# Twelve pieces of unread matrix products in a replaced order of work, in an attention and gMLP kernel on one core

## The chip, the cores and the metric

The kernel runs on one core of a Trainium2 chip. The metric is the device time of one execution in microseconds (us), as the median of several. A profile of one further execution gives the span from the first instruction to the last one and the time of every instruction on every engine.

The engines are named as in the profile: PE is TensorE (its matmuls), PEld the loading of PE's weights, DVE is VectorE, ACT is ScalarE, POOL is GpSimd and SP is SyncE, which here issues transfers only. Each engine runs its own list of instructions strictly in the order in which the program gives them, and waits on semaphores for the others.

## The reference

Inputs are q, k and v of shape 4 x 8 x 768 x 64 (batch, heads, positions, head size) and the weights of a gated MLP. For each head the 768 keys are cut into 24 chunks of 32. Of each chunk the smallest and largest value per dimension give an upper bound on the score of a query:

```python
ub = np.sum(np.maximum(q[:, :, :, None, :] * k_min[:, :, None, :, :], q[:, :, :, None, :] * k_max[:, :, None, :, :]), axis=-1)
causal = pos[:, None] // chunk >= np.arange(nc)[None, :]
ub = np.where(causal, ub, -1000000000.0)
top_chunks = np.argsort(ub, axis=-1)[..., -top_k:]
```

Each query then attends, causally, only to the keys of its six best chunks, with an ordinary softmax. The 128 queries of the first tile reach four chunks at most, so that none of theirs is ever left out. The eight heads side by side (512 numbers a position) go through the MLP: `h = max(x @ w_in, 0)`, the second half of `h` normalised per position and mixed over positions by a 768 x 768 matrix plus a bias, multiplied by the first half, and then by `w_out`. The output is 4 x 768 x 512 in float32.

## The kernel before

The work is done for 16 pairs of heads, p = 0 to 15, four for each of the four batches; the pair's two heads lie on the two halves of the 128 partitions. After the four pairs of a batch b comes the MLP of that batch. All of it is cut into some 1400 named pieces, each a few instructions on one engine. `work_list` (L251 to L461) lists each piece with its engine (or the two that may do it), a planner's cost in us, the pieces that it comes after, and the buffers that it takes new or uses. A function `k_<name>` writes each piece's instructions. The pieces that matter here, in the order of one pair:

- `load` (L626) brings k, q, v in; `cast` (L635) makes them 16 bits wide; `turn` (L648) transposes k or q on PE, six matmuls of 128 columns; `kT`, `qT` (L661, L674) copy the result out of PSUM and `qp` (L679) makes max(-q, 0). From the fifth pair on transfers on SP do the transposing.
- `ext` (L666): two DVE reductions that give each chunk's largest and smallest key values.
- `bounds` (L692): PE forms the upper bounds of all queries with all chunks, for six tiles of 128 queries and both heads, in matmuls of 24 columns. For the first six pairs (`EARLY`) a product of `big` and `far`, which marks the chunks that lie ahead, is added as one more matmul; for the others DVE adds it in `ub`.
- `ub`, `top`, `leave` (L704 to L725): the bounds are copied out, DVE finds the eight largest of each row, and marks what is left out. `top` reads the bounds of tiles 1 to 5 only. In `leave` the first tile's threshold is a constant which lies between the mark of a chunk ahead and any bound.
- `pk`, `mx` (L770, L792): scores with keys across, and their largest per chunk by DVE reductions, so that the softmax knows what to subtract. For the first three pairs part of that is folded: `kd` on POOL, `fd`, `fi`, `fb` on PE and `fr` on ACT.
- `minus`, `kept`, `shift`, `turn_bias`, `bT`: the bias of each query and chunk, transposed by PE in six matmuls that use half of the array's rows each (L826).
- `probs`, `ex` (L843, L867): scores with queries across plus the bias on PE, exponential on ACT, in six slices. `cut` (L874) on POOL clears what lies ahead in the diagonal blocks, once for each head.
- `weigh` (L880) multiplies by v on PE; `av`, `sum`, `inv`, `norm` (L888 to L916) copy out and divide; `turn_x`, `xT` transpose for the MLP.

The MLP of a batch is `hv`, `vr`, `bn`, `rstd`, `vn` (the half that is normalised), `hu`, `uT` (the other one), `mix`, `ms` or `plus`, `gT` (mixing over positions and gating), and `og`, `oe`, `od` (last product, copy out, store).

Two things set the order. **The order of the pieces** comes from `Work.order` (L114 to L215), which runs while the program is built: it plays the work through with the costs of the list, and on each engine takes of the pieces that are ready the one with the lowest number in the table `RANK`. `WHERE` gives one letter for each piece that could go to two engines. **PE's two ways of use**: pieces of the kinds in `TILED` (L100) have matmuls on 64 rows, two of which run side by side; the others use all 128 rows. The planner adds 0.095 us where PE goes from one kind to the other.

PSUM holds three double buffers of tag `two` and two single ones of tag `mg`. A piece that takes a buffer waits until the last reader of the one before is done.

At the start the first load of k goes to ACT's queue and all others to SP's. POOL makes constants (`ident`, `far`, `rows`), DVE fills others (`clear`, `zero`, `small`, `halves`), and PE has nothing to do until the first `turn`.

Of the kernel before, what the change touches and what calls it, by code (L numbers as in the profile page):

```python
# [16 lines left out]
P = 128  # L17
# [15 lines left out]
0 9 100 7 13 10 5 1 28 103 118 168 128 124 256 303 296 313 298 327 425 450 446 421 430 435 398 407 417 422 403 411 388  # L33
396 381 391 2 11 3 12 4 44 14 16 20 23 17 19 21 27 32 35 38 43 39 41 54 29 22 25 24 31 40 47 55 61 71 66 37 42 48 51
60 56 65 68 77 102 112 115 119 125 130 136 159 163 146 151 135 143 150 155 145 171 178 152 177 180 186 196 199 209 214
15 49 8 34 36 82 58 63 79 107 46 57 52 123 132 139 147 140 148 149 154 72 70 75 73 84 89 105 138 144 153 158 87 90 101
108 114 116 111 160 165 172 179 183 187 193 202 204 213 224 218 230 195 200 216 221 217 242 250 228 253 258 263 270
274 284 292 6 26 18 53 80 113 30 33 45 50 64 69 74 81 85 93 99 98 94 106 129 59 83 88 157 161 169 173 184 190 197 194
76 78 95 109 122 126 120 141 208 215 236 239 247 254 257 262 271 276 278 281 266 267 268 273 269 300 306 283 290 308
315 332 335 347 354 67 92 62 86 96 134 104 110 133 142 91 117 97 227 231 237 240 249 244 243 255 166 170 191 238 251  # L40
164 176 252 259 198 201 203 207 282 285 261 293 299 311 314 317 324 334 338 343 349 328 331 337 342 330 336 344 358
364 350 369 377 382 387 392 414 418 121 156 127 174 175 233 162 167 181 188 182 185 189 205 212 219 222 223 225 220
229 232 235 245 260 264 294 302 275 279 304 312 287 291 288 295 241 319 339 353 360 365 372 393 399 423 439 420 427
374 380 413 416 415 483 488 408 497 506 514 526 529 552 131 192 137 211 246 305 226 272 277 234 286 297 301 309 345
310 346 321 352 307 318 323 355 359 322 326 409 419 362 371 340 348 432 437 361 442 452 465 467 475 479 493 500 509
518 507 511 535 549 489 492 520 561 568 513 566 575 582 584 587 595 210 265 206 248 329 402 280 333 341 289 316 351
356 366 367 368 375 370 378 379 384 389 434 440 405 412 445 455 397 400 401 404 386 394 385 459 468 482 486 548 578
593 600 574 585 606 610 571 592 627 630 647 658 667 626 668 682 691 714 739 749 320 357 325 373 390 454 363 424 429
395 460 521 527 534 539 536 538 541 572 463 470 477 558 562 461 480 554 559 504 510 496 499 487 494 577 583 594 634
641 649 656 655 662 672 678 687 693 663 669 681 685 686 723 730 713 728 733 742 746 748 763 383 438 376 428 474 543  # L50
443 503 517 433 498 532 545 551 576 557 553 555 580 519 523 530 540 547 591 601 636 645 565 569 666 670 612 617 588
680 688 705 708 711 719 731 745 736 741 761 767 718 725 751 756 765 776 783 759 781 789 798 812 818 827 406 471 410
481 528 590 564 605 611 544 598 623 628 635 637 643 639 652 657 609 615 622 651 659 701 710 750 754 638 648 675 679
625 632 770 777 790 804 807 817 822 832 838 811 825 857 863 829 845 831 836 842 889 897 847 905 917 930 935 939 949
516 550 522 567 619 785 631 664 674 644 673 683 694 698 717 699 720 702 732 690 697 703 715 721 768 772 760 764 753
757 860 867 738 743 794 876 882 909 915 938 944 950 953 942 947 962 970 977 984 960 965 975 996 1003 1002 1013 1020
1028 1032 1066 1077 581 665 573 653 726 795 696 727 735 707 737 766 769 778 786 784 782 780 808 775 787 799 846 856
868 873 773 803 788 793 883 890 885 895 814 899 920 972 978 985 989 1004 1011 1000 1006 993 997 1019 1023 1034 1039
1038 1050 1057 1043 1055 1061 1071 1079 1084 1093 661 774 654 734 821 888 779 813 834 771 802 844 852 861 866 865 880
881 918 879 886 898 900 907 982 986 1007 1010 896 904 954 958 995 999 922 1024 1030 1049 1052 1062 1069 1067 1074 1078  # L60
1091 1083 1087 1075 1082 1094 1100 1098 1109 1113 1092 1105 1117 1122 1133 1136 1144 797 837 792 826 892 927 864 913
925 874 919 951 956 963 964 971 966 968 979 911 923 936 1045 1056 967 974 1017 1025 991 994 941 946 914 931 1080 1104
1115 1127 1131 1138 1142 1148 1153 1151 1156 1166 1175 1157 1163 1172 1179 1158 1198 1203 1165 1202 1208 1211 1213
1216 1222 810 853 816 870 926 1108 983 1005 1018 990 1014 1031 1037 1044 1047 1060 1064 1048 1072 1026 1033 1041 1170
1174 1095 1101 1042 1051 1059 1065 1159 1164 1103 1107 1076 1182 1194 1197 1201 1218 1221 1238 1245 1207 1227 1236
1240 1205 1224 1251 1254 1256 1263 1269 1250 1270 1274 1276 1279 1281 1288 908 1012 912 952 1063 1112 1040 1073 1088
1054 1081 1099 1110 1118 1160 1121 1150 1134 1168 1111 1120 1126 1185 1196 1191 1200 1181 1186 1116 1137 1183 1189
1114 1123 1177 1206 1212 1235 1237 1242 1248 1267 1272 1252 1257 1258 1264 1255 1261 1266 1271 1275 1283 1287 1280
1285 1290 1291 1293 1295 1302 1305 436 444 447 441 449 458 478 484 491 451 457 462 469 476 485 456 464 473 502 505 515
524 560 570 546 563 537 426 431 490 495 466 472 512 531 501 508 542 556 448 453 525 533 586 599 602 613 596 604 607  # L70
640 579 589 597 616 642 650 660 671 618 624 692 724 603 608 621 633 629 646 709 729 614 620 676 700 706 712 722 677
684 689 695 704 716 740 747 806 755 762 801 744 752 758 791 800 823 835 841 848 805 815 820 796 809 828 824 833 839
819 830 843 855 859 872 875 906 903 894 878 891 840 850 862 869 851 858 849 854 871 884 877 887 902 910 893 901 916
924 932 957 973 980 988 998 933 940 948 959 955 976 981 992 928 934 943 1008 945 961 1016 1053 987 1001 1027 1058 921
929 937 969 1036 1046 1068 1022 1029 1035 1009 1015 1021 1070 1086 1089 1090 1097 1106 1085 1096 1102 1119 1125 1130
1124 1129 1147 1145 1149 1155 1141 1146 1152 1128 1135 1139 1132 1140 1143 1162 1169 1178 1184 1204 1190 1209 1214
1195 1154 1167 1192 1199 1210 1217 1176 1188 1215 1219 1173 1180 1187 1193 1161 1171 1229 1232 1233 1220 1225 1234
1243 1249 1260 1223 1228 1239 1226 1230 1244 1259 1265 1268 1246 1253 1262 1231 1241 1247 1277 1284 1286 1292 1298
1299 1300 1304 1306 1273 1278 1282 1289 1294 1296 1297 1301 1303 1307 1309 1311 1310 1315 1317 1308 1312 1314 1313
1318 1320 1316 1321 1324 1319 1325 1329 1323 1326 1332 1335 1340 1336 1334 1337 1344 1346 1347 1348 1322 1328 1333  # L80
1341 1345 1351 1327 1331 1338 1343 1330 1339 1349 1353 1342 1350 1358 1361 1362 1352 1355 1365 1354 1357 1366 1356
1359 1363 1369 1375 1379 1360 1368 1371 1364 1370 1374 1367 1372 1377 1380 1385 1387 1376 1382 1384 1373 1378 1381
1389 1393 1394 1386 1391 1392 1383 1388 1390
"""
WHERE = """
AAAAGAGAGVGVGAAVAGAGAGVVAGAGAGAVVVVVAVAVAAAAAVVAVGGGGVGGAAVAAAAAAAAAAAVVAVAVVAAVAAVVGGGGGVVAAAAA
# [3 lines left out]
class Work:  # L90
# [8 lines left out]
    DELAY = {"PE": 0.25, "DVE": 0.17, "ACT": 0.18, "POOL": 0.14, "SP": 0.0}  # L99
    TILED = ("pk", "probs", "bounds", "turn_bias", "fd", "fb")  # L100
# [12 lines left out]

    def order(self):  # L114

        pieces, n = self.pieces, len(self.pieces)
        users, slot, freed_at, done_at = {}, {}, {}, {}
        slots = {tag: [None] * k for tag, k in self.bufs.items()}
        then, todo, ready_at, begun = [[] for _ in range(n)], [0] * n, [0.0] * n, [False] * n
        for i, (_, _, _, after, new, old, _) in enumerate(pieces):  # L120
            for b in new + old:
                users[b] = users.get(b, 0) + 1
            for a in after:
                then[self.index[a]].append(i)
                todo[i] += 1
        rank, where = [int(x) for x in RANK.split()], iter(WHERE.replace("\n", ""))
        engine = dict(P="PE", V="DVE", A="ACT", G="POOL", S="SP")
        assert len(rank) == n
        for i, (name, on, _, after, new, old, dma) in enumerate(pieces):
            if len(on) > 1:  # L130
                e = engine[next(where)]
                on = {e: on[e]}
# [934 lines left out]
```

## Time and profile before

| | before |
|---|---|
| median of 3 runs | 249.05 us (248.89 to 249.26) |
| the profiled execution's own time | 248.22 us |
| its span | 246.5 us |
| PE busy, matmuls | 224.9 us of it, 3780 instructions |
| DVE busy | 206.5 us, 512 instructions |
| ACT busy | 191.9 us, 298 instructions |
| POOL busy | 165.9 us, 209 instructions |
| moved by DMA | 35.51 MB |

A busy time is the sum of stretches in which the engine had an instruction under way. Matmuls overlap, so PE can be busy throughout and still have pauses between starts. In a row of the timeline or of the groups, "L807 DVE" is line 807 of the kernel before and its engine, "cmax<-two" the tile written and the one read, "x2" the count. In the chain of waits a row gives the start, the length, and what the end of the program waited for at that time.

### The profile page before, as it was taken

The page shows a single profiled execution, that of the slowest core. Times are in us where ns is not written, and L with a number is a line of the kernel's source. Part 1 is how long each engine was busy: PE and PEld are TensorE (multiplying, and loading weights), DVE is VectorE, ACT ScalarE, POOL GpSimd, SP SyncE. Part 2 cuts the span into 40 slices and gives each one's busy share as a digit, 9 for nine tenths or more (in the row PEclk, how much of TensorE's full clock was granted, in tenths as well). Part 3 has the DMA queues.
Part 4 walks back from the last instruction along what each step waited for, and adds up shares of the span by engine and source line. Part 5 has one row for each costly group of instructions (what it writes and reads, how often), then busy time and mean ns, then how long its engine had stood idle before and what let it go on. Part 6 is the DMA issues. An engine that isn't in the chain of part 4 may idle for free.

```text
span 246.5 us, 9019 instructions
## 1 busy us (share of the span) xinstructions
PE 224.9 (91%) x3780; PEld 144.6 (59%) x3780; DVE 206.5 (84%) x512; ACT 191.9 (78%) x298; POOL 165.9 (67%) x209
## 2 busy tenths in 40 slices
PE   0898778878999999999999999999999999999993
PEld 0656457666755675666665576666745566645551
DVE  4799999999999999799998997899998853349670
ACT  3598887979998999587859897897679969767312
POOL 8879749887785377999965929999926147402160
PEclk9999999999999999999999999999999999999999
DMA  7969996699999949484899997128900010350005
GB/s 189 325 186 201 257 242 127 122 164 241 168 186 235 216 82 187 89 170 112 190 161 271 175 200 125 34 75 140 268 22 19 0 36 0 105 188 0 0 28 227
DMA packets 93895, 35.51 MB, mean 144 GB/s; under 512 B 86208, under 2 KB 90144, under 8 KB 93856
## 3 DMA queue, kind: packets, MB, share of 16 engines
q1 hardware_dynamic: 91568, 31.81, 61.9%
q0 software_dynamic: 2016, 2.75, 6.5%
q8 instruction: 29, 0.48, 0.8%
q10 hardware_dynamic: 272, 0.39, 0.5%
q14 instruction: 10, 0.08, 0.1%
HBM read 24.77 MB, written 6.29 MB: 126 GB/s over the span
## 4 chain that ended last, share of the span: by engine, by line
PE 48%; DVE 28%; ACT 14%; DMA 4%; issue 3%; POOL 2%; DVEq 0%; ACTq 0%
DVE cmax L807 11%; PE mg L1001 11%; ACT pr L871 8%; PE mg L1024 6%; PE mg L885 5%; PE two L856 4%; PE mg L937 3%; PE two L863 3%; DVE stats L954 3%; DVE ext L671 3%; PE two L786 3%; DVE top L715 2%; PE mg L990 2%; DMA k<-in_k_dram 2%; DVE cmax L801 2%
## 5 line engine op out<-in xcount | busy, mean ns | idle before, releaser
L871 ACT ACTIVATE pr<-two 128x1024 f16<-128x1024 f32 (+1 forms) x96 | 85.3, 934 | 5.4 <-PE two L863 4.8
L807 DVE TENSOR_REDUCE cmax<-two 128x24 f32<-128x768 f32 (+4 forms) x104 | 85.3, 843 | 3.5 <-PE two L735 2.0
L856 PE MATMUL two<-qT,kT 64*128 64x128 f16 (+3 forms) x384 | 40.5, 258 | 5.4 <-ACT bT L835 1.9
L863 PE MATMUL two<-bT,member 64*128 64x128 f16 (+1 forms) x512 | 39.7, 233 | 0.0
L877 POOL TENSOR_SCALAR_AFFINE_SELECT pr<-pr 128x768 f16<-128x768 f16 x32 | 27.9, 886 | 9.1 <-ACT pr L871 9.0
L1019 POOL TENSOR_TENSOR vr<-tmp,uT 128x384 f16<-128x384 f32 x27 | 24.5, 922 | 11.9 <-DVE tmp L1012 11.8
L671 DVE TENSOR_REDUCE ext<-kT 128x24 f16<-128x768 f16 x32 | 29.5, 936 | 1.9 <-ACT kT L617 1.7
L1001 PE MATMUL mg<-wsT,vn 128*128 128x384 f16 x168 | 30.2, 327 | 0.0
L856 PEld LDWEIGHTS <-kT 64*128 64x128 f16 x384 | 19.9, 94 | 17.2 <-issue 15.1
L863 PEld LDWEIGHTS <-member 64*128 64x128 f16 x512 | 25.7, 94 | 5.1
L885 PE MATMUL mg<-v,pr 128*128 128x65 f16 x672 | 25.9, 194 | 0.7 <-POOL pr L877 0.5
L786 PE MATMUL two<-kT,qT 64*128 64x384 f16 (+4 forms) x182 | 24.6, 280 | 1.4 <-ACT pr L871 0.5
L885 PEld LDWEIGHTS <-pr 128*128 128x128 f16 x672 | 23.1, 98 | 3.6 <-issue 1.0
L1001 PEld LDWEIGHTS <-vn 128*128 128x128 f16 x192 | 17.7, 98 | 12.2 <-issue 0.6
L990 PE MATMUL mg<-xT,w_in_sb 128*128 128x384 f16 x112 | 22.4, 328 | 0.0
L907 POOL TENSOR_TENSOR x<-av,rc 128x768 f16<-128x768 f32 x11 | 16.2, 1469 | 8.8 <-DVE rc L900 4.9
L732 PE MATMUL two<-kT,qT 64*128 64x128 f16 x192 | 19.6, 221 | 2.3 <-ACT qT L617 1.0
L1024 PE MATMUL mg<-w_out_sb,vr 128*128 128x512 f16 x84 | 20.8, 380 | 0.0
L937 PE MATMUL mg<-w_in_sb,xT 128*128 128x512 f16 x84 | 20.3, 380 | 0.4 <-DVE o L619 0.4
L889 ACT COPY av<-mg 128x390 f32<-128x390 f32 x32 | 15.6, 500 | 6.2 <-PE mg L885 6.0
L954 DVE BATCH_NORM_STATS2 stats<-vr 128x6 f32<-128x512 f32 x24 | 16.6, 692 | 4.0 <-ACT vr L942 2.9
L735 PE MATMUL two<-half_ahead,ident 64*128 64x64 f16 x192 | 19.8, 193 | 0.0
(113 smaller groups left out, 496.8 us busy)
## 6 DMA issues: line engine op xcount, KB each, us to landing
q<-in_q_dram SPq DMA_DIRECT2D x16, 384.0 KB, 6.4
v<-in_v_dram SPq DMA_DIRECT2D x16, 384.0 KB, 5.7
out_dram<-o SPq DMA_DIRECT2D x24, 256.0 KB, 2.1
k<-in_k_dram SPq DMA_DIRECT2D x15, 384.0 KB, 5.7
vr<-in_moe_w_spatial_dram POOLq DMA_DIRECT2D x6, 192.0 KB, 5.6
w_in_sb<-in_moe_w_in_dram POOLq DMA_DIRECT2D x4, 256.0 KB, 8.8
w_out_sb<-in_moe_w_out_dram POOLq DMA_DIRECT2D x4, 128.0 KB, 4.5
k<-in_k_dram ACTq DMA_DIRECT2D x1, 384.0 KB, 4.7
```

What stands on the lines that cost most here:

```text
L671: nc.vector.tensor_reduce(held["ext", p][:, m], src, axis=AX.X, op=Alu.min if m else Alu.max, negate=(m == 1))
L786: mm(t[:, h, o:o + before], lhsT=qT[rows[h], c], rhs=kT[rows[h], a * CH:a * CH + before], start=True, stop=True)
L807: nc.vector.tensor_reduce(tops(p)[:, i // 2, :, i % 2, a:z], held["two", (p, u)][:, :, o:o + n].rearrange("p h (c e) -> p h c e", e=CH), a ...
L856: mm(t[:, h, z:z + n * P], lhsT=kT[rows[h], keys], rhs=qT[rows[h], i * P:(i + n) * P], start=True, stop=False)
L863: mm(d, lhsT=member[rows[h], r, keys], rhs=bT[rows[h], m * P:(m + w_) * P].rearrange("c (m s) -> c m s", s=P), start=False, stop=(n == 1 o ...
L871: nc.scalar.activation(out=held["pr", p][:, :, c0:c0 + n], in_=held["two", (p, "e", c0)][:, :, 0:n], func=Act.Exp, scale=scale)
L877: nc.gpsimd.affine_select(out=d, in_=d, compare_op=Alu.is_ge, fill=0.0, base=0, channel_multiplier=-1, pattern=[[0, NT], [1, P]])
L885: mm(a[:, i, :], lhsT=pr[:, at[t, i]:at[t, i] + P], rhs=vp[:, h * NT + t, :], start=(t == 0), stop=(t == i))
L937: mm(t, lhsT=held["xT", b][:, ko, i * P:(i + 1) * P], rhs=w_in_sb[:, ko, DH:2 * DH], start=(ko == 0), stop=(ko == NDO - 1))
L990: mm(t, lhsT=w_in_sb[:, ko, db * P:(db + 1) * P], rhs=held["xT", b][:, ko, s * HS:(s + 1) * HS], start=(ko == 0), stop=(ko == NDO - 1))
L1001: mm(t, lhsT=held["vn", b][:, si, db * P:(db + 1) * P], rhs=wsT[:, si, s * HS:(s + 1) * HS], start=(si == 0), stop=(si == NT - 1))
L1024: mm(t, lhsT=held["vr", ("g", b)][:, ko, i * P:(i + 1) * P], rhs=w_out_sb[:, ko, :], start=(ko == 0), stop=(ko == KO - 1))
```

## The change

- **Unread products.** A piece `spark` on DVE fills a tile of 128 x 512 with ones. Twelve pieces `warm`, each three matmuls of 128 rows by 512 columns with these ones, write PSUM buffers of tag `mg` that nobody reads.
- **The order.** `RANK` is a new table, and now holds each piece's place itself: nothing is played through any more. `WHERE` is new as well. A buffer goes to the one of its tag that has been out of use longest. A few planner costs differ (`norm`, `plus`, `gT`, `bn`, `rstd1`, `bounds`).
- **The first tile's bounds.** For tile 0 only the product of `big` and `far` is made, for all pairs; the three products with the keys are left out.
- **`turn_bias`.** Where both neighbours on PE use all rows, its matmuls take all 128 rows too (pairs 1, 4, 10 and 14).

PE's list begins so (before on the left, changed on the right):

```
turn 0 k            warm 11, 7, 2, 6
turn 0 q            turn 0 k
pk 0,0              warm 4
pk 0,1              turn 0 q
bounds 0            warm 8, 5
turn 2 k            pk 0,0
fd 0,1              bounds 0
fd 0,0              pk 0,1
turn 1 q            turn 2 k, fd 0,1, fd 0,0
fi 0,1              warm 0, 9
fb 0,1              fi 0,1
```

`warm` 3, 10 and 1 follow at places 25, 29 and 31 of PE's list (counted from 0), between pieces of pairs 1 and 2. SP's list begins with q of pair 0, then k and q of pair 2, q and k of pair 1, and only then v of pair 0, which stood second before. On DVE `ub` of pairs 0 and 1 is new, and `ub` of pairs 3 and 4 has gone to ACT. `norm` of pairs 7 and 11 goes from POOL to DVE, `norm` of 13, 14 and 15 from DVE to POOL. Some pieces of the last two MLPs change engines as well.

```diff
-    for i in range(NT):   # k_bounds
-            each = [(big, far[:, i])] * (p < EARLY) + [(qT[:, c], x[:, 0]), (qp[:, c], x[:, 0]), (qp[:, c], x[:, 1])]
+            each = [(big, far[:, i])] * (p < EARLY or i == 0) + [(qT[:, c], x[:, 0]), (qp[:, c], x[:, 0]), (qp[:, c], x[:, 1])] * (i > 0)
...
+    w.add(("spark",), {"DVE": 0.3}, -10)
+    for x in range(WARM):
+        w.add(("warm", x), {"PE": 0.64}, -9 + 0.4 * x, after=[("spark",)], new=[("mg", ("warm", x))])
...
+    def k_spark(e):
+        nc.vector.memset(spark, 1.0)
+
+    def k_warm(e, x):
+        t = new("mg", ("warm", x), [P, 512], F32)
+        for n in range(3):
+            mm(t, lhsT=spark[:, 0:P], rhs=spark, start=True, stop=True)
...
+        rank, where = [int(x) for x in RANK.split()], iter(WHERE.replace("\n", ""))
...
+        for (name, on, _, _, _, _, _), at in zip(pieces, rank):
+            result[at] = name, engine[next(where)] if len(on) > 1 else next(iter(on)), at
...
+                free = [(-1 if x is None else last[x], k) for k, x in enumerate(tenants) if x is None or users[x] == 0]
+                slot[b] = min(free)[1]
...
-                mm(t[:, g, m * D:(m + 1) * D], lhsT=bias[slot["bias", p]][r, 4 * m:4 * m + 4, :].rearrange("p g c -> p (g c)"), rhs=ident[r, r], start=True, stop=True)
+                if p in whole:
+                    r, c = c, r
+                mm(t[:, g, m * D:(m + 1) * D], lhsT=bias[slot["bias", p]][r, 4 * m:4 * m + 4, :].rearrange("p g c -> p (g c)"),
+                   rhs=ident[r, c] if p in whole else ident[r, r], start=True, stop=True)
```

## The prediction

> **What bounds the kernel now.** I read the page first, then the busy time by stretches, then the chain of waits in order of time, and last the timeline of the first 16 us.
>
> ```profile
> span 246.5 us, 9019 instructions
> PE 224.9 (91%) x3780; PEld 144.6 (59%) x3780; DVE 206.5 (84%) x512; ACT 191.9 (78%) x298; POOL 165.9 (67%) x209
> PEclk9999999999999999999999999999999999999999
> ```
>
> The profiled execution took 248.22 us, 1.7 more than its span. The median of the runs is 249.05, 0.83 above it. I make the sum against 248.22 and add 0.83 at the end. PE is the busiest, but over the whole span this says little, since stages differ. Columns: us of the stretch, then busy time of PE, PEld, DVE, ACT, POOL.
>
> ```profile
> 0.00:7.80 7.80, 1.46 (x12) 1.20 (x12) 3.02 (x20) 2.92 (x4) 6.29 (x19) 1.00 0.79 217
> 7.80:20.00 12.20, 10.68 (x249) 7.62 (x250) 11.79 (x26) 9.43 (x14) 9.97 (x13) 1.00 0.84 231
> 20.00:40.00 20.00, 16.13 (x378) 11.58 (x375) 19.23 (x57) 18.02 (x25) 14.75 (x23) 1.00 1.09 232
> 40.00:60.00 20.00, 16.64 (x454) 12.84 (x450) 19.96 (x54) 17.33 (x26) 16.54 (x23) 1.00 0.87 155
> 60.00:80.00 20.00, 19.78 (x310) 12.65 (x308) 19.18 (x42) 18.18 (x29) 14.32 (x19) 1.00 1.20 201
> 80.00:100.00 20.00, 19.72 (x381) 13.20 (x378) 19.40 (x53) 19.09 (x32) 12.84 (x14) 1.00 0.92 164
> 180.00:200.00 20.00, 19.92 (x234) 10.99 (x233) 15.86 (x38) 18.99 (x33) 7.22 (x8) 1.00 0.11 22
> ```
>
> There are three stages. Until 7.8 us all wait for the first k. From 7.8 to 60 DVE is the bound: of 52.2 us it is idle for 0.41 + 0.77 + 0.04 = 1.2, while PE is idle for 8.8. From 60 on PE is busy almost throughout, in the first 40 us of it together with DVE and ACT. Whatever shortens PE's work before 60 us is worth nothing there, unless it brings work to DVE earlier.
>
> **The clock of PE.** The page's clock row and the clock column of the stretches (the 1.00) show full speed throughout. The timeline contradicts them at the start:
>
> ```profile
> 1.02 0.70 DVE L576 MEMSET member<- 128x768 uint32 x1 [1.02 <-PEq L1051]
> 6.14 0.82 PE L652 MATMUL mg<-ident,k 128*128 128x128 f16 x6 [6.14 <-DVE k L619]
> 7.00 0.80 ACT L617 COPY kT<-mg 128x768 f16<-128x768 f16 x1 [1.06 <-PE mg L652]
> 7.69 0.81 ACT L617 COPY qT<-mg 128x768 f16<-128x768 f16 x1
> 7.83 1.81 DVE L671 TENSOR_REDUCE ext<-kT 128x24 f16<-128x768 f16 x2 [1.75 <-ACT kT L617]
> 8.55 0.29 PE L732 MATMUL two<-kT,qT 64*128 64x128 f16 x2 [0.95 <-ACT qT L617]
> 9.55 1.81 DVE L795 TENSOR_REDUCE cmax<-two 128x24 f32<-128x768 f32 x2
> 12.29 0.80 PE L652 MATMUL mg<-ident,q 128*128 128x128 f16 x6
> 15.05 0.50 PE L652 MATMUL mg<-ident,k 128*128 128x128 f16 x6
> ```
>
> The same six transposes take 0.82 at 6.14, 0.80 at 12.29 and 0.50 at 15.05. So PE is slow until some time between 13.1 and 15.05; it needed at most 15.05 - 8.55 = 6.5 us of nearly unbroken work, counted from its last long pause. The difference of 0.32 is 0.053 for 128 columns, so 0.21 for 512. A 512-column matmul at full speed takes a quarter of the 0.86 below, 0.215; slow, I estimate 0.43.
>
> ```profile
> 10.01 0.64 PE two L702 x48
> 112.59 0.97 PE mg L1024 x4
> 151.79 1.08 PE mg L1001 x6
> 153.43 0.44 PE two L702 x36
> 160.54 0.77 PE mg L885 x21
> 163.40 0.66 PE mg L885 x21
> 229.76 0.97 PE two L1001 x6
> 239.29 0.86 PE mg L1024 x4
> ```
>
> **Unread products and the first stage.** Each piece is 3 x 0.215 = 0.65 us at full speed, 1.28 slow (estimates). `spark` fills 512 halves; `clear` fills 1536 in 0.70, so about 0.3. It ends at 1.3, and DVE's fills, late by as much, end long before DVE's cast of k at 5.5. PE can start at 1.5. Four pieces stand before the first transposes, one between k's and q's, two before `pk` 0,0.
>
> Say the clock rises after 6.3 us of work, the upper end from the rows: at 7.8. Then the four pieces end at 1.5 + 5.1 = 6.6, the k transposes at 7.25 (before 6.96 with their tail), and kT is copied from 7.4 instead of 7.00: +0.4 for `ext`. `warm` 4 and q's transposes follow until 8.5, qT is copied from 8.7 to 9.5, `warm` 8 and 5 end at 9.8, and `pk` 0,0 gives DVE its first `mx` at 10.35 instead of 9.55: **+0.8**. If the clock rises by 5.7, the four pieces end before 6.14; k's transposes take 0.5, kT comes 0.3 earlier, and `warm` 8 and 5 then hold `pk` until 8.8, which at full speed still delivers by 9.35: **-0.2**. So ahead of DVE the pieces gain 0.2 or lose 0.8. What they give later is that PE, fast from then on, feeds DVE without pauses. DVE's idle time from 7.8 to 60 is 1.2 us, and no more than that can go. The five later pieces, 3.2 us of PE, lie where PE waits for `fr` or for DVE, with 8.8 us idle to hide them; without that cover they would cost their 3.2. `bounds` 0 now precedes `pk` 0,1 and waits for the second `ext`; behind it on PE stands only `pk` 0,1, for which DVE's `mx` comes after `ub`.
>
> ```profile
> L619 DVE COPY ub<-two 128x288 f32<-128x288 f32 x2 | 0.9, 446 | 0.0
> L907 POOL TENSOR_TENSOR x<-av,rc 128x768 f16<-128x768 f32 x11 | 16.2, 1469 | 8.8 <-DVE rc L900 4.9 <-ACT bT L835 3.3 <-ACT pr L871 0.3
> L907 DVE TENSOR_TENSOR x<-av,rc 128x768 f16<-128x768 f32 x5 | 5.0, 996 | 0.1
> ```
>
> Two `ub` of 0.45 come to DVE and two leave it within the stage: nothing. I take +0.8 for the start and -0.8 of the 1.2 idle: **0**, with ends of -1.4 and +0.8. v of pair 0 is now behind four more loads on SP's queue, but POOL's cast of it stands later as well, and its first reader is `weigh` 0 after 30 us.
>
> Here a page of the Trainium skill can be weighed. "TensorE: Matmul & The Clock Gate", section "Part 1: The HAM clock gate", says that the array runs at half speed until a free-running window of about 3.4 us has been busy. By that rule the pieces from 1.5 us on would open the gate between 4.9 and 8.3, and the start would be worth -0.2 to about +1.1 in place of +0.8. The rows agree on the halving (0.82 against 0.50); that 8.55 to 13.1 did not suffice here is slower than the section's typical 4 us.
>
> **First tile's bounds.** For pairs 0 to 5, 6 of 48 matmuls go: 6/48 x 0.64 = 0.08 each, all in the stage where PE has time: 0. For the other ten, 4 of 36: 4/36 x 0.44 = 0.05 each, **-0.5** in the stage where PE is full.
>
> **Fewer changes of PE's use.** A group followed by the other kind lasts longer: `og` 0.97 against 0.86, `mix` 1.08 against 0.97, `weigh` 0.77 against 0.66, so 0.11 for a change. Counting the two orders, PE changes 172 times before and 168 times after; from `turn_x` of pair 2 on (58.7 us) 140 times and 128. The 12 that go, 1.3 us, lie almost all between 59 and 127 us, and in 60 to 100 DVE and ACT are as full as PE. I count half: **-0.65** (0 to -1.3). `turn_bias` on all rows is in the count: six matmuls of 64 columns one after another, where two and two ran side by side: by 64/128 of the 0.056 of a fast transpose (0.50 for six, with their tail) a loss below 0.1 each.
>
> **The end of pair 15.** PE waits there twice:
>
> ```profile
> 211.52 2.50 POOL pr L877 x2
> 214.06 0.84 PE mg L885 x21
> 214.90 3.48 PE mg L1024 x16
> 218.41 0.70 DVE o L619
> 219.15 1.89 PE mg L937 x8
> ```
>
> `weigh` 15,1 waits for the two `cut`, because slice 512 of `probs` 15 came last; 1.33 us lie between the starts of 15,0 (212.73) and 15,1 (214.06) where 0.66 would do. The new order puts that slice before both `weigh` of pair 14, but then slice 1024 comes late, and ACT's exponential of it ends about 0.4 too late by the same counting: -0.3. Then `norm` 15 goes to POOL, 1.47 for 1.00, and only three `og` (2.6 us) instead of four cover it. From `weigh` 15,1 on: copy, sum and reciprocal end after 1.85 as before, `norm` after 3.4, the transposes start after 3.5 and the copy of xT ends after 4.9; the fourth `og` runs beside that copy. `hv` 3 starts after 4.95 instead of 219.15 - 214.06 = 5.09: -0.15. Together **-0.5** (+0.2 to -0.8). From `hv` 3 on both orders run PE without a pause, and the last store follows a copy on ACT in both.
>
> **Other waits.**
>
> ```profile
> PE two L856 <- DVE cmax L807: 0.9, 2, 0.5
> PE two L786 <- DVE cmax L807: 0.2, 1, 0.2
> ```
>
> These are the first and the last of six rows on which PE waits after 55 us, 3.0 us in all. A new order of every engine may have none of them or as many again: 0, ends -3 and +3.
>
> **Sum.** 0 - 0.5 - 0.65 - 0.5 = -1.65. The profiled execution would come to 248.22 - 1.65 = 246.6, the median to **247.4**. Its own range, by half of the ends: 246.1 to 248.5.
>
> **Rivals.**
> 1. *The products stand in the way* (slower). If the clock rises late, all seven early pieces run slow: four end at 6.6, k's transposes at 7.25, `warm` 4 and q's at 9.2, `warm` 8 and 5 at 11.7, `pk` 0,0 delivers at 12.5 instead of 9.55: DVE is 3.0 us late, in a stage in which it is the bound. That gives 247.4 + 3.0 = 250.4, about 249.9 with some idle time regained. It outweighs the gains from a rise after some 9.5 us on. For it: counted from the first matmul (6.14) the rise took up to 8.9 us, which from 1.5 would be 10.4. Against: PE paused for 0.9 us in between, and the new work has no such pauses. In it the change also doesn't do what it says, since PE's first real work is as slow as before.
> 2. *DVE and ACT take the gain back.* If in the stretch from 60 to 100 DVE (19.2 and 19.4 of 20) sets the pace, and `norm` 7 and 11 add 2 x 1.0 to it after 100, neither bounds nor changes of use count. Left is -0.5 at the end, less 0.3 for DVE: 248.9.
> 3. *The whole gain.* The clock rises by 5.7 (-0.2), DVE's 1.2 idle goes, all changes count (another -0.65), and a third of the 3.0 us of waits goes with the order: 247.4 - 0.2 - 1.2 - 0.65 - 1.0 = 244.4; with half of these extras 245.9.
>
> **Chances.** Forecast 0.45, rival 1 0.22, rival 2 0.13, rival 3 0.20. A difference below 0.2%, 0.5 us, can hardly be told from none. Faster by more: 0.63 (forecast and rival 3, but for a little), within: 0.15, slower: 0.22. The range of 245.0 to 250.0 takes in the greater part of the rivals.
>
> **What would show it.** In the changed profile: the first k transposes take 0.5 and not 0.8 us, and the first `mx` starts between 9.3 and 10.4. DVE is idle for under 0.5 us from there to 60. `turn_x` 2 comes at 58 to 59 (58.7 before). PE's waits after 55 us sum to some 3 us. From `turn_x` 2 to `hv` 3,0, 160.4 us before, it should be 158 to 159. The forecast is wrong if the first `mx` starts after 11, or if the stage after 60 has waits of PE over 5 us.

## The result, and the profile after

| | before | after |
|---|---|---|
| median, same chip, 4 runs each | 249.16 us (248.89 to 249.43) | 251.5 us (251.44 to 252.14) |
| ratio after to before | | 1.010, 95% interval 1.008 to 1.012 |
| the profiled execution's own time | 248.22 us | 251.44 us |
| its span | 246.5 us | 249.4 us |
| DVE busy from 7.8 to 60 us, of 52.2 | 50.98 us | 50.55 us |

The change makes the kernel 1.0% slower; 247.4 us had been forecast. The rows of the page of after that answer to those of before, with the row of the clock:

```profile
span 249.4 us, 8906 instructions
PE 233.1 (93%) x3740; PEld 146.9 (59%) x3740; DVE 211.0 (85%) x516; ACT 192.0 (77%) x296; POOL 166.8 (67%) x208
PEclk9999999999599999999999999999999999999999
```

The clock row, all nines before, has a 5 in its eleventh slice: near 65 us the array runs at half clock. The busy time by stretches shows the same place (columns as in the prediction: us, then PE, PEld, DVE, ACT, POOL, granted clock, DMA share, GB/s):

```profile
7.80:20.00 12.20, 11.93 (x248) 7.40 (x247) 11.68 (x29) 8.37 (x12) 8.48 (x12) 1.00 1.12 257
20.00:40.00 20.00, 18.00 (x414) 12.29 (x413) 19.29 (x57) 19.23 (x27) 15.63 (x24) 1.00 0.87 180
40.00:60.00 20.00, 16.70 (x421) 12.94 (x421) 19.58 (x51) 17.46 (x27) 16.19 (x22) 1.00 0.95 154
60.00:80.00 20.00, 16.30 (x236) 11.51 (x233) 15.06 (x33) 13.73 (x21) 9.75 (x13) 0.83 1.03 194
80.00:100.00 20.00, 19.91 (x368) 13.19 (x367) 19.65 (x53) 19.41 (x35) 13.44 (x18) 1.00 1.12 170
```

In the stretch from 60 to 80 every engine is less busy than before: PE 16.30 for 19.78, DVE 15.06 for 19.18, ACT 13.73 for 18.18. The waits of PE after 55 us, the first two of six rows (engine, tile and line that waits, what it waits for: us in all, times, longest):

```profile
PE mg L551 <- DMA vr<-in_moe_w_spatial_dram: 2.8, 2, 2.0
PE mg L551 <- ACT bT L780: 0.5, 1, 0.5
```

L551 is `turn_ws`, which transposes the spatial weights of the MLP; each such piece reads a column block of all six loads of `vr`. The timeline of PE shows the first one, `turn_ws` 4, in three parts (in square brackets PE's pause just before, and what ended it):

```profile
60.30 0.34 PE L775 MATMUL two<-ident,bias 128*128 128x64 f16 x6
61.18 0.23 PE L551 MATMUL mg<-ident,vr 128*128 128x128 f16 x1 [0.54 <-ACT bT L780]
62.20 0.34 PE L551 MATMUL mg<-ident,vr 128*128 128x128 f16 x3 [0.79 <-DMA vr<-in_moe_w_spatial_dram]
64.55 0.40 PE L551 MATMUL mg<-ident,vr 128*128 128x128 f16 x2 [2.01 <-DMA vr<-in_moe_w_spatial_dram]
```

One transpose runs, three more when the next load has landed, and the last two at 64.55. Of the pauses, 0.54 us is put down to a copy on ACT and 2.8 us to the loads. PE keeps to its list, so all that stands behind `turn_ws` 4 waits with it. In before the first of these pieces started at 63.48 and found all six loads landed:

```profile
63.48 0.51 PE L609 MATMUL mg<-ident,vr 128*128 128x128 f16 x6
```

Two things have moved toward each other. In PE's list the first `turn_ws` now stands two pieces behind `weigh` 3,0, where it stood six behind; and the weights arrive later. In the chain of waits of after (start, length, what the end waited for) the last load is the longest row of all:

```profile
55.04 9.47 DMA vr<-in_moe_w_spatial_dram
```

Issued at 55.04, it landed at 64.51; in before it was issued at 54.94 and landed at 61.27. The DMA table gives the median of all six from issue to landing, 5.6 us before:

```profile
vr<-in_moe_w_spatial_dram POOLq DMA_DIRECT2D x6, 192.0 KB, 8.5
```

The last three loads leave back to back from 53.95 on. And the bias broadcast `b_load`, 384 KB on SP's queue, has gone from 19.36 us, where nothing waited for it, into the very stretch of these loads. The row of SP's timeline before, and then after:

```profile
19.36 0.70 SPq L592 DMA_DIRECT2D bB<-in_moe_b_spatial_dram  x1
```

```profile
51.12 1.08 SPq L534 DMA_DIRECT2D bB<-in_moe_b_spatial_dram  x1
```

Behind the wait the clock falls. The trace records it at half from 62.58 to 69.40; the stretch of 3.4 us ahead of the fall and the two at half clock, in the same columns as above:

```profile
59.16:62.58 3.42, 2.04 (x39) 1.46 (x38) 2.97 (x9) 1.49 (x3) 0.48 (x2) 1.00 1.16 205
62.58:65.99 3.41, 1.44 (x28) 1.25 (x30) 0.35 (x2) 0.80 (x1) 0.82 (x1) 0.50 1.08 217
65.99:69.40 3.41, 3.41 (x55) 2.87 (x51) 1.98 (x8) 2.09 (x3) 1.60 (x2) 0.50 1.01 175
```

So PE first does nothing and then does its work at half speed; the next `turn_ws` takes 0.83 for 0.51. `turn_x` of pair 2 comes at 57.85, 0.9 earlier than before (58.74), and `hv` 3,0 at 221.99, 2.84 later (219.15). Between these two marks the new order loses 0.9 + 2.84 = 3.7 us.

### The profile page after: what moved, and what is told of

It is laid out like the page before. It is cut to its first block, busy times and chain, and to the rows that moved or that the text cites. A ratio compares the mean times of both kernels' runs of the same rounds, so it can differ in the third digit from the quotient of the medians.

```text
span 249.4 us, 8906 instructions
## 1 busy us (share of the span) xinstructions
PE 233.1 (93%) x3740; PEld 146.9 (59%) x3740; DVE 211.0 (85%) x516; ACT 192.0 (77%) x296; POOL 166.8 (67%) x208
## 4 chain that ended last, share of the span: by engine, by line
PE 59%; ACT 20%; DVE 9%; DMA 6%; issue 2%; POOL 2%; DVEq 0%; ACTq 0%; POOLq 0%
PE mg L946 10%; ACT pr L816 8%; PE mg L882 7%; PE mg L830 6%; PE mg L969 6%; PE two L801 5%; PE two L808 4%; PE mg L935 4%; DVE cmax L749 4%; DMA vr<-in_moe_w_spatial_dram 4%; ACT vn L925 3%; PE two L728 3%; PE mg L509 2%; DMA k<-in_k_dram 2%; PE two L674 2%
## 5 line engine op out<-in xcount | busy, mean ns | idle before, releaser
L816 ACT ACTIVATE pr<-two 128x1024 f16<-128x1024 f32 (+1 forms) x96 | 84.4, 931 | 9.2 <-PE two L808 8.2
L801 PE MATMUL two<-qT,kT 64*128 64x128 f16 (+3 forms) x384 | 41.0, 261 | 2.9 <-ACT pr L816 1.8
L946 PE MATMUL mg<-wsT,vn 128*128 128x384 f16 x168 | 30.7, 327 | 0.7 <-DVE tmp L957 0.5
L728 PE MATMUL two<-kT,qT 64*128 64x384 f16 (+4 forms) x182 | 25.9, 284 | 1.9 <-ACT pr L816 1.1
L830 PEld LDWEIGHTS <-pr 128*128 128x128 f16 x672 | 23.6, 99 | 3.7 <-issue 1.5
L852 POOL TENSOR_TENSOR x<-av,rc 128x768 f16<-128x768 f32 x12 | 18.0, 1498 | 9.3 <-DVE rc L845 7.7
L935 PE MATMUL mg<-xT,w_in_sb 128*128 128x384 f16 x112 | 21.8, 327 | 0.0
L559 ACT COPY o<-mg 128x512 f32<-128x512 f32 x17 | 9.9, 597 | 11.7 <-PE mg L969 11.7
```

The costliest lines, as they stand in the source:

```text
L728: mm(t[:, h, o:o + before], lhsT=qT[rows[h], c], rhs=kT[rows[h], a * CH:a * CH + before], start=True, stop=True)
L801: mm(t[:, h, z:z + n * P], lhsT=kT[rows[h], keys], rhs=qT[rows[h], i * P:(i + n) * P], start=True, stop=False)
L816: nc.scalar.activation(out=held["pr", p][:, :, c0:c0 + n], in_=held["two", (p, "e", c0)][:, :, 0:n], func=Act.Exp, scale=scale)
L830: mm(a[:, i, :], lhsT=pr[:, at[t, i]:at[t, i] + P], rhs=vp[:, h * NT + t, :], start=(t == 0), stop=(t == i))
L935: mm(t, lhsT=w_in_sb[:, ko, db * P:(db + 1) * P], rhs=held["xT", b][:, ko, s * HS:(s + 1) * HS], start=(ko == 0), stop=(ko == NDO - 1))
L946: mm(t, lhsT=held["vn", b][:, si, db * P:(db + 1) * P], rhs=wsT[:, si, s * HS:(s + 1) * HS], start=(si == 0), stop=(si == NT - 1))
```

## The experiments

Theory: `turn_ws` stands too early for the landing of the weights, and the broadcast delays the landing. Rivals: the unread products cost the time, or the new order is worse in itself.

**The broadcast early.** In the changed kernel only `b_load` goes back to its old place in SP's list.

```diff
 load 3 v
+b_load
 load 4 k
...
-b_load
 load 7 q
```

> The changed kernel with one transfer moved: the broadcast load of the bias (393 KB to 128 partitions) goes back ahead of k of pair 4 in SP's list, where the kernel before has it. Theory (the broadcast at 51 us takes transfer time from the six loads of the spatial weights, whose last one lands at 64.5 instead of 61.3, and PE waits for it): the last weight load lands near 61.5, PE waits under 1 us for it, its clock stays at full speed from 60 to 80, and the median is 246.5 to 248.5. Rival A (PE's list has the transposes of these weights too early, whatever the transfers do): PE still waits 2 to 3 us there, median 250 to 251.5. Rival B (the loss is spread over the new order): 251 to 252.

Measured: 249.92 us, ratio to before 1.0049 (1.0019 to 1.0079). About half of the loss remains, and so does the wait, as rival A had it (the time is just under its range). The two marks of the theory, a last load near 61.5 us and a wait under 1 us, both failed:

```profile
PE mg L551 <- DMA vr<-in_moe_w_spatial_dram: 2.5, 2, 2.0
```

The last load lands at 63.39 instead of 64.51, but PE reaches `turn_ws` 4 earlier as well, at 60.41. The clock is at half for one window of 3.41 us instead of two. The broadcast is a part of the cause and not all of it; in this profile the loads take 7.1 us in the median without it, between 5.6 in before and 8.5 in after.

**The broadcast late, in the kernel before.** Only `b_load` is moved, to the place that it has in the changed kernel.

```diff
-b_load
 load 4 k
...
+b_load
 load 7 k
```

> The kernel before with the same load moved the other way, to just before k of pair 7 on SP's queue. Theory: the last weight load lands some 3 us later than 61.3, of which 2.2 us are slack before PE's first transpose of these weights (63.5); PE waits about 1 us or a little more, median 249.8 to 251. Rival A (the order on PE matters, not the load): no change, 248.9 to 249.4.

Measured: 250.1 us, ratio 1.0064 (1.0045 to 1.0084). The time is the one that the theory expected, but not for its reason: PE does not wait for the weights at all. The last load lands at 63.81, 2.5 us later than in before, of which 0.9 is a later issue, and the old order reaches `turn_ws` 5 only at 64.58. The clock stays full. A row of the timeline, and one of the stretches:

```profile
64.58 0.51 PE L612 MATMUL mg<-ident,vr 128*128 128x128 f16 x6
```

```profile
60.00:80.00 20.00, 18.46 (x320) 12.18 (x318) 18.27 (x40) 17.07 (x27) 13.52 (x19) 1.00 1.27 191
```

Late, the broadcast costs 0.6% even where nothing waits for the weights. The profiled execution, at 251.02 us, is 0.9 above the median, so its times tell less than the ratio: `turn_x` 2 is 0.9 late in it (59.65), but 0.7 of that stands already at the first transposes (6.83 for 6.14), long before the broadcast leaves at 51.63. In the stretch from 60 to 80 PE loses 1.3 us of busy time against before, and one row of the timeline holds it:

```profile
78.12 0.34 PE L789 MATMUL two<-kT,qT 64*128 64x384 f16 x2 [1.25 <-DVE stats L957]
```

The chain of waits leads from there back over DVE and `kept` on POOL (at 75.46) to a load of k, issued at 66.72 and 5.18 us under way. Whether the broadcast made that load late was not tried.

**No products.** The version with the early broadcast without `spark` and the twelve `warm`.

```diff
-WARM = 12
+WARM = 0
-    w.add(("spark",), {"DVE": 0.3}, -10)
```

> e1 without the twelve unread products and without their tile of ones; the rest of the order as it is. If the products move the start by the 0.4 us by which the first copy of k came sooner, and keep PE fast from 4.5 us on: slower than e1 by 0.7 to 1.5 us. If DVE hides them: within 0.3 us of e1. If they stand in the way, as the first rival of the prediction had it: faster than e1.

Measured: 251.63 us, ratio 1.013 (1.007 to 1.019). Without the products it is 1.7 us slower than with them (249.92): the first transposes take 0.82 again, and the clock is recorded as full only from 17.8 us on, with the products from 5.3. The two intervals just overlap, but the pair of ten runs each below gives the same sign without an overlap. The rival that blames the products has fallen.

**Products alone.** The kernel before with `spark` and four `warm` ahead of the first transposes, and nothing else.

```diff
+        warm = [("spark",)] + [("warm", x) for x in range(WARM)]
+        return [(n, "PE" if n[0] == "warm" else "DVE", 0.0) for n in warm] + result, slot
-        return result, slot
```

> The kernel before, with only the tile of ones and the first four products (12 matmuls) ahead of PE's first transposes; its order otherwise untouched. If a fast PE at the start is worth what the first copy of k gains: 0.4 to 1.2 us faster than before, 248.0 to 248.7. If DVE and ACT hide it: 249.0 to 249.3.

Measured: 248.38 us, ratio 0.9996 (0.9968 to 1.0023). The interval reaches from 0.8 us faster to 0.6 slower, so no difference is shown; by the medians (248.38 and 248.82 on this chip) it would be 0.4 faster. The clock is full from 5.3 us and the first transposes take 0.51:

```profile
1.51 4.62 PE L580 MATMUL mg<-spark 128*128 128x512 f16 x12 [1.51 <-DVE spark L575]
6.14 0.51 PE L665 MATMUL mg<-ident,k 128*128 128x128 f16 x6
58.56 0.51 PE L935 MATMUL mg<-ident,x 128*128 128x128 f16 x6
```

`turn_x` 2, the last of these rows, comes 0.18 earlier than before.

**The transposes later.** In the changed kernel, its broadcast still late, `turn_ws` 4, 3 and 5 and their copies are set later by some 3 us of PE's work; nothing is added or left out. PE's list:

```diff
 weigh 3,0
 turn_bias 4
-turn_ws 4
 pk 6,0
 probs 4,0
 pk 6,6
 weigh 3,1
-turn_ws 3
 pk 6,4
 probs 4,2048
 pk 5,6
-turn_ws 5
+turn_ws 4
 probs 4,512
+turn_ws 3
 pk 5,3
+turn_ws 5
```

> The changed kernel with the late broadcast kept, but with the first three of the six transposes of the spatial weights (turn_ws 4, 3, 5, and their copies) set behind some 3 us of other PE work of pairs 3 to 6 that had stood behind them. Theory, second half (PE's list puts these transposes 3 us too early for weights that land at 63.4 to 64.5): PE waits under 0.5 us for the weights, its clock does not fall, and most of the loss goes: 247.5 to 249. Rival (PE would find nothing to do there, since DVE and ACT are not ready with the work set ahead): the wait moves to other semaphores, median above 250.5.

Measured: 247.8 us, ratio 0.9975 (0.9954 to 0.9996). The whole loss is gone. This profile is 1.7 us behind that of after at `turn_x` 2 already (59.56), so its times can be compared only with each other: the last load lands at 65.52, and PE, which has other work until then, comes to `turn_ws` 4 at 66.25. The timeline, then the only wait of `turn_ws` that is left (for a copy, not for a load), and the stretch:

```profile
66.25 0.51 PE L551 MATMUL mg<-ident,vr 128*128 128x128 f16 x6
```

```profile
PE mg L551 <- ACT wsT L554: 1.0, 1, 1.0
```

```profile
60.00:80.00 20.00, 18.06 (x325) 12.37 (x324) 18.81 (x40) 16.94 (x26) 12.43 (x17) 1.00 1.15 196
```

The clock is 1.00 here and stays full to the last slice. The place of three pieces, with their copies, makes the difference between 1.0% slower and 0.25% faster.

**Both moved.** The early broadcast and the later transposes together. It was timed on two chips, the second time beside the version without products below.

> e1 and e5 together: broadcast early and transposes later. If each half alone removes the wait, this is like the better of them: 247 to 248.5, and faster than the kernel before by 0.3 to 0.8%. If the rest of the new order loses too: 249 or more.

> The version with both moved once more, beside the one without the products on the same chip: 247.8 us, the clock full from 7 us to the end.

Measured: 247.82 us, ratio 0.9978 (0.9952 to 1.0004), and on the second chip 247.47 us, ratio 0.9955 (0.9932 to 0.9977). With the transposes later, the early broadcast adds nothing that these intervals can tell (0.9978 against 0.9975 on one chip). Against the early broadcast alone (1.0049) the later transposes are worth 0.7%.

**Both moved, no products.**

```diff
-WARM = 12
+WARM = 0
-    w.add(("spark",), {"DVE": 0.3}, -10)
```

> The changed kernel with the broadcast of the bias early and the transposes of the spatial weights later, as in the version with both moved, but without the twelve products and the fill that feeds them. Theory: the products are worth the 1.7 us by which the version with the early broadcast got slower without them; then the time is 247.8 + 1.7 = 249.5 us, and the granted clock rises to full only 10 us or later. Rival: most of that 1.7 us came from the wait for the weights and the half clock behind it, and without that wait the products are worth 0.3 us or less: 247.8 to 248.1 us.

Measured: 249.38 us, ratio 1.0016 (0.9979 to 1.0054), on the chip on which the version with them took 247.47. So the products are worth 1.9 us by the medians and 1.5 by the ratios, about the 1.7 of the pair with the stall, and the rival, that most of that came from the wait, has fallen. (Three of the ten runs without products have a mean granted clock of 0.986 to 0.993, so they lost some windows of the clock somewhere; the median of the other seven is 248.83, still 1.4 above.) `turn_x` 2 without the products, and then with them:

```profile
60.30 0.51 PE L866 MATMUL mg<-ident,x 128*128 128x128 f16 x6
```

```profile
57.87 0.51 PE L867 MATMUL mg<-ident,x 128*128 128x128 f16 x6
```

The gain is made ahead of 60 us, 2.4 us of it; 1.3 are left at `hv` 3,0 (219.81 and 218.53). How it is made stands in the waits of DVE from 7.8 to 60 us. Without the products they have this row, and with them it is missing:

```profile
DVE cmax L742 <- PE two L707: 2.0, 2, 1.1
```

L707 is `fb`, PE's last step of the folded scores, and L742 the `mx` that reads them. The clock is recorded as full only from 18.25 us on without the products and from 5.56 with them, and DVE, which is the bound of this stage, is idle for 52.2 - 48.73 = 3.5 us of it without and 52.2 - 50.58 = 1.6 with them. The pair with the stall shows the same, 1.9 us of this wait and none. In before DVE waits only 0.2 us for `fb`: the old order left little for a faster PE to give.

Without products the new order reaches `turn_x` 2 later than the old one (60.30 against 58.74): in these profiles it is the worse one ahead of 60 us unless PE is fast from the start.

**Products in the wait.** The changed kernel with six more `warm` ahead of `turn_ws` 4, to keep PE busy while the weights come, so that the wait stays and the half clock goes.

```diff
 turn_bias 4
+warm 12 to 17
 turn_ws 4
```

> The changed kernel with six more unread products (18 matmuls, 3.9 us at full speed) just ahead of turn_ws 4, where PE waits for the weights. They add no useful work and cannot bring the weights. If the half clock after the wait (62.6 to 69.4) costs time by itself: the clock stays full and the median falls by 1 to 2.4 us, to 249 to 250.5. If the wait alone is the loss: 251.5 to 252.

Measured: 251.47 us, ratio 1.010 (1.006 to 1.014). It settles nothing. In the profiled execution (254.18) the products waited themselves, until ACT had copied out the buffer that they take, so the clock fell all the same (one window), and then they ran at half speed in the way of the rest. In the other four runs, 250.56 to 252.62, the mean granted clock is 0.996 to 1.000, less than one window lost, and they are not clearly faster than the version without these products; but there 3.9 us of products stand in the way. The row of the waits, and that of the timeline:

```profile
PE mg L510 <- ACT av L835: 1.7, 1, 1.7
```

```profile
62.96 6.61 PE L510 MATMUL mg<-spark 128*128 128x512 f16 x18 [1.74 <-ACT av L835]
```

**One set of transposes early, in the kernel before.** The kernel before with the late broadcast and `turn_ws` 5 ahead of `weigh` 3,0, with its copy; the other way round than the cure above. (With it 74 buffers of tag `mg` change places between the two.)

```diff
 pk 5,1
+turn_ws 5
 weigh 3,0
...
 pk 6,0
-turn_ws 5
 pk 6,6
```

> The kernel before with the late broadcast, and besides with one set of transposes of the spatial weights, the first (turn_ws 5), set ahead of weigh 3,0, some 3.3 us earlier. Theory (the place of the transposes against the landing of the weights makes the loss): PE waits some 2.5 us for the weights at 61 to 64 us, the clock may fall to half for one or two windows behind it, and the time is 250.1 + 2.5 = 252.6 us, up to 253.6 with the clock. Rival (the wait is regained behind it, and the loss of the changed kernel is its other order): 250.1 us, as with the late broadcast alone.

Measured: 251.8 us, ratio 1.0116 (1.0048 to 1.0183): 1.7 more than the late broadcast alone by the medians, on another chip and with intervals that overlap. In the profiled execution the wait is there, but short, because the last load landed at 62.32 in it:

```profile
PE mg L630 <- DMA vr<-in_moe_w_spatial_dram: 1.4, 2, 1.0
```

Its four runs scatter with the clock: 249.66 (this one) and 251.21 us with a mean granted clock of 1.000, 252.40 and 253.29 with 0.993 and 0.992. A mean of 0.993 is what one window at half clock gives, 0.5 x 3.41 / 249 = 0.7%. By the means of two and two the one window goes with 2.4 us; that is four runs, and a longer wait may be behind both.

**The bounds alone.** The kernel before without the first tile's bounds with the keys, which nothing reads.

```diff
-            each = [(big, far[:, i])] * (p < EARLY) + [(qT[:, c], x[:, 0]), (qp[:, c], x[:, 0]), (qp[:, c], x[:, 1])]
+            each = [(big, far[:, i])] * (p < EARLY or i == 0) + [(qT[:, c], x[:, 0]), (qp[:, c], x[:, 0]), (qp[:, c], x[:, 1])] * (i > 0)
```

> The kernel before with only the first tile's bounds left out (76 matmuls of 24 columns fewer; the first tile's values are read by nobody). By the prediction's term 0.5 us faster, 248.3 to 248.6 beside 248.8 to 249.1; if DVE and ACT hide it: no difference.

Measured: 248.99 us, ratio 1.0021 (1.0001 to 1.0042). The half microsecond did not come; if anything it is slower.

## Why the prediction was wrong

The step that failed is the one under **Other waits**: "A new order of every engine may have none of them or as many again: 0, ends -3 and +3." Nothing of the new lists was looked up for it. It stood for the very thing that decides, where the new lists put a piece that waits for a transfer against the time at which that transfer lands. The new place of `b_load`, past twelve entries of SP's list, and the last three loads, which POOL now issues in a row, could be read from the lists, as could `turn_ws` 4 two pieces behind `weigh` 3,0. The landing times of before (61.27 for the last) would have left `turn_ws` 4, reached at 61.2, just covered; but in the new order the last load landed at 64.51, and at 63.39 with the broadcast out of the way. By the runs the term was +3.1 us (the ratio of 1.010 against 0.9975 with the transposes later, 1.25% of 249), and by the two profiles +4.4 (164.1 against 159.7 from `turn_x` 2 to `hv` 3,0): at its own end of +3 or past it. The rows of waits quoted for it were those of before, which could not hold a wait that only the new order has. The ends of +3 and -3 did not reach the prediction's own range either: 246.1 to 248.5 is, to within 0.1, half of the ends of the other terms; with this one half of the ends is 244.7 to 250.0. And no rival was a wait for a transfer: the 0.22 for slower stood for the products. With the stall taken away the kernel is 0.6 us faster (0.25% of 249) where -1.65 had been forecast; this 1.0 and the 3.1 are the 4.1 us by which the forecast missed.

The others, in the order of the prediction:

- **First stage, 0 (ends -1.4 and +0.8).** In the profile of after `turn_x` 2 came 0.9 earlier, inside the ends, and the markers held: k's transposes took 0.51, and the first `mx` started at 9.79, between 9.3 and 10.4.

```profile
1.51 4.25 PE L509 MATMUL mg<-spark 128*128 128x512 f16 x12 [1.51 <-DVE spark L504]
6.08 0.51 PE L594 MATMUL mg<-ident,k 128*128 128x128 f16 x6 [0.32 <-DVE k L561]
6.42 0.81 PE L509 MATMUL mg<-spark 128*128 128x512 f16 x3
9.79 0.96 DVE L737 TENSOR_REDUCE cmax<-two 128x24 f32<-128x768 f32 x1 [0.52 <-PE two L677]
```

  Part of that is luck of the execution. The prediction had worked out a rise of the clock by 5.7 us and one at 7.8; in the six profiles with the twelve products it lies between 4.55 and 7.33. With the rise up to 5.56 (three of them) the first `mx` starts at 9.72 to 9.81, where 9.35 had been forecast. With the rise at 7.11 and 7.33 (later transposes, and both moved) k's transposes take 0.75 and 0.85, and the first `mx` starts at 10.55 and 10.65, outside the marker. `turn_x` 2 lies at 57.78 to 57.87 in the three early ones, at 58.44 to 59.56 in the other three and at 58.42 to 59.65 in the five profiles of the old order, so the 0.9 by itself is within the scatter.

  DVE's idle time from 7.8 to 60 did not fall below 0.5 as forecast; it is 52.2 - 50.55 = 1.65 for 1.22. But 1.22 is the idle time of the old order. The new order without products has 3.5, and the products take 1.9 of that away. So the mechanism, a fast PE that feeds DVE without pauses, held; its price had been read from the order that was to be replaced.
- **First tile's bounds, -0.5.** Not seen: 1.0021 alone. Four matmuls fewer in each of ten groups did not move the end.
- **Fewer changes of use, -0.65.** With the stall gone, `turn_x` 2 to `hv` 3,0 takes 159.7 with the transposes later, 160.1 and 160.7 with both moved and 159.5 without products besides, for 160.4 before. That is between +0.3 and -0.9 for this term, the bounds and pair 15 together, where -1.65 had been forecast. Profiles of the old order with the same changes of use have 159.9 (products alone) and 161.3 (bounds alone), so a term of this size cannot be told in single profiles.
- **The end of pair 15, -0.5.** From `weigh` 15,0 to `hv` 3,0 after takes 221.99 - 216.25 = 5.74, before 219.15 - 212.73 = 6.42: -0.68. The two `weigh` now run without a pause, as one row:

```profile
216.25 1.49 PE L830 MATMUL mg<-v,pr 128*128 128x65 f16 x42
```

  What the later exponential costs ahead of it was not measured.
- **Rival 1, products in the way (0.22).** It had the sign but not the reason. The products do hold up `pk` 0,0, even with the clock up early: with both moved the first `mx` starts at 9.81 with them and at 9.53 without. But without them the kernel is slower.
- **Rival 3, the whole gain (0.20).** With the stall taken away the kernel is 0.2% to 0.45% faster than before, where the forecast had 0.7% and this rival 1.3% to 1.9%. And what gain is shown lies ahead of 60 us, from the clock, not in the steady stage where the forecast had put it.
- **What would show it.** In the profile of after PE's waits after 55 us sum to 4.8 for the 3 forecast, just short of the 5 at which the forecast called itself wrong; the mark did not count the half clock that follows a wait. The mark that spoke was `turn_x` 2 to `hv` 3,0: 164.1 for 158 to 159.

What remains open is how the loss divides. PE stood for 3.3 us at `turn_ws` 4. From 64.55 to 69.40 it then worked at half clock, at most 2.4 us of extra time if all of it was bound by the array. The two sum to 5.7, more than the loss, so a part was regained behind them or the array did not bound all of it; the one experiment that was to part them did not. The mean granted clocks of the timed runs point both ways. Of the four runs of after, the one whose mean (0.993) leaves room for one window at half took 251.45 us, no less than two with two windows (0.986; 251.44 and 251.54). Of the four without products and with the early broadcast, those with 0.993 took 250.25 and 250.75, those with 0.984 took 252.5 and 253.1; there a longer wait can be behind both.

## What to carry to other kernels

Where an order is written out for every engine, check each piece that waits for a transfer against the landing of that transfer in the new order, and count every transfer that was moved into the same stretch; a piece that stands a few places too early holds up all that stands behind it. Behind a wait of some 3 us the clock of PE fell for one or two windows of 3.4 us here; what that costs beyond the wait is not shown. Products that bring the clock up early are worth what the order makes of a fast PE: 1.5 to 1.9 us in the new order, where DVE otherwise waits for PE, and no difference that could be shown in the old one, where it hardly does (with four of the twelve products). And idle times and waits that are read from the profile of one order are no price for another.

## What the runs showed of the hardware

**The clock goes by windows.** Each time between two recorded changes of the clock is a multiple of 3.413 us: in after 58.03 at full (17 windows), then 6.83 at half (2). PE's busy time in these windows shows what it took. In before the window ahead of the rise at 14.83 was full of work; the two ahead of it, with 1.46 and 2.86 us of it, did not suffice:

```profile
4.59:8.00 3.41, 1.46 (x12) 1.20 (x12) 0.73 (x2) 1.84 (x3) 2.76 (x3) 1.00 1.18 300
8.00:11.41 3.41, 2.86 (x92) 2.64 (x94) 3.41 (x6) 1.61 (x3) 2.97 (x4) 1.00 1.06 352
11.41:14.83 3.42, 3.40 (x25) 1.55 (x26) 3.19 (x14) 3.39 (x5) 2.65 (x4) 1.00 0.60 101
```

(The clock column reads 1.00 here although the transposes of the same windows take 0.82 and 0.80; before the first record of the clock it says nothing.) In all profiles of this study the least busy window behind which the clock rose had PE busy for 3.04 us, in after from 1.14 to 4.55, and the busiest behind which it did not rise had 2.86. With products the rise came between 4.55 and 7.33 us, without between 12.2 and 18.3. The grid lies differently against the start of each execution, and a scatter of up to one window can come from that.

**Some 2 us of work in a window can be too little to keep it.** In the middle of the kernel the clock fell behind windows in which PE was busy for 2.04 us (59.16 to 62.58 in after, quoted above), 1.61, 1.21 and 1.07. It stayed behind others with 1.89 to 2.15, so the busy time of the records is not quite what is counted. The Trainium skill, "TensorE: Matmul & The Clock Gate", section "Part 1: The HAM clock gate", has the same free-running window of 3413 ns and lets the clock fall after an idle one. The grid of these traces agrees with the window's length; the fall does not need a wholly idle window here, as the row with 2.04 of 3.42 shows.

**The six loads on POOL's queue.** Their median from issue to landing is 7.4 to 8.5 us in the three profiles with the new order and the late broadcast, and 6.1 to 7.1 in the five with the new order and the early one. With the old order it is 6.2 in the two with the late broadcast and 5.5 to 6.9 in the three with the early one. Only the new order and the late broadcast together stand clearly apart. The new order issues its last three loads in a row, the old one its second to fourth; whether that matters was not tried.
